# Summing h11 in PSUM: the first product's bank is copied into the second's, and the second product accumulates on the copy

## The chip, the cores and the metric

The kernel runs on one core of one Trainium2 chip. The metric is the device time of one execution in microseconds (us), the median of several runs.

## The reference

Attention over channels is followed by a feed-forward network. For each of 4 batches, q, k and v are 6080 x 256 arrays.

```python
qn = q / (norm(q, axis=1) + 1e-06)          # norm over the 6080 rows
kn = k / (norm(k, axis=1) + 1e-06)
s = kn.transpose(0, 2, 1) @ qn / tau        # 256 x 256 in each batch
a = softmax(s)                              # over the last axis
x = (v @ a).reshape(24320, 256)
h = x @ w_in                                # w_in 256 x 2048
g = maximum(0.01 * h, h)
out = g @ w_out                             # w_out 2048 x 256
```

The result is 24320 x 256. Everything is float32 outside the chip.

## The kernel before, in words

**What is multiplied.** The kernel first works out, for each batch, the product of the attention matrix with w_in (W). Then h comes from v and W with the seven products of Strassen's scheme in Winograd's form, and out comes from g and w_out. Each float32 operand is split into a high and a low half, and each product is three matmuls (`PASSES`): high by high, low by high, high by low. For the first batch the halves are 32 bits wide, later they are float16.

**Tiles and pairs.** The columns of v are worked in 24 tiles (`i`), six in each batch, of 2 x 512 columns and, for the last two of a batch, 2 x 496. In each tile there are eight pairs (`p`). A pair computes four blocks of h, which are named C11, C12, C21 and C22. Tile 0 has an order of its own, tiles 1 to 14 are the conventional tiles of this document, and tiles 15 to 23 (`FAST`) are worked by another function, `fast_slot`.

**One conventional pair.** TensorE does seven block products of three matmuls each (`block_product`, L1193) into two PSUM banks, x and z, of which there is one each:

```python
block_product(i, p, x, A11, "B11", True, False)
h11 = taken(i, x)
block_product(i, p, y, A12, "B21", True, True)
...
add(i, h11, y)
...
block_product(i, p, x, S2, "T2", False, False)
h12 = taken(i, x)
...
block_product(i, p, z, S1, "T1", True, False)
```

In these tiles y is bank z too. The text calls the products by their second operands: B11, B21, T2, T1, T3, T4, B22, in that order. B11, T2, T3 and T4 run into bank x one upon the other; B21 into z; T1 into z from zero; and B22 upon T1. `taken` (ScalarE, L1230) copies bank x into an SBUF tile h. `add` (VectorE, L1224) adds bank z to h. So h11 is the copy of x after B11 plus z after B21; h22 is the copy of x after T3 plus z after T1; h12 is the copy of x after T2 plus z after B22; and C21 is read from x itself after T4. `leaky` (ScalarE L1207 twice, or L1207 and L1213 for C21; VectorE L1217) makes g and its two halves.

**The order of the work.** Each engine's order is written out by hand: `run` and `in_order` keep instructions of one engine in the order of the program. The products of g by w_out of the pair before (`ffn_out`, L1604, 24 matmuls in a pair, six for each of C11, C22, C21 and C12) are put between the block products by `out(n)`, n matmuls at a time: 5, 5, 8 and the remaining 6. Work of other parts of the kernel (scores and norms of later batches, W, splits of v, conversions) waits in lists, and `slot(list, room)` takes entries from the front of a list as long as their written lengths fit in the room. The room that is left over in a slot of ScalarE or VectorE is carried to the next in tiles 6 to 14, up to 0.6. In a conventional pair VectorE has slots of 1.45 (between the h11 addition and C11), 2.2 (between C11 and the h22 addition), 1.45 (between the h22 addition and C22) and 0.8 (at the end).

**fast_slot.** Tiles 15 to 23 copy bank x into bank z after B11 (L1517, ScalarE) and let B21 accumulate on the copy. The matmuls of the pair before that stand between are `out(6)`.

Of the kernel before, what the change touches and what calls it, by code (L numbers as in the profile page):

```python
# [14 lines left out]
AF = mybir.ActivationFunctionType  # L15
# [22 lines left out]
G_SCALE = 2.0**-19  # L38
# [5 lines left out]
def channel_attention_ffn(  # L44
# [17 lines left out]
    nc = tc.nc  # L62
# [10 lines left out]
    widths = [TW] * (N // TILE)  # L73
# [4 lines left out]
    NT = len(widths)  # L78
    NPAIR = NF // 2
    WPB = NT * NPAIR  # L80
    NTILES = B * NT
    T16 = NT
    LEAN = 2
    UNIT = 3
    FAST = range(NTILES - NT - EARLY, NTILES)
# [9 lines left out]
    def bank(tag, bufs=1):  # L95
        return psum.tile([P, TW], F32, name="ps_" + tag, tag=tag, bufs=bufs)
# [37 lines left out]
    issued = {}  # L134

    @contextmanager
    def in_order(*engines):
        with ExitStack() as stack:
            for e in engines:
                if e in issued:  # L140
                    stack.enter_context(tc.issue_after(issued[e].ins))
            yield

    def run(engine, fn, *args):
        with in_order(engine):
            issued[engine] = ins = fn(*args)
        return ins

    def f32(ap):
        return ap if ap.dtype == F16 else ap.bitcast(F32)  # L150

    def pair_type(i):
        return F16 if i >= T16 else F32R
# [105 lines left out]
    class Scores:  # L259
# [95 lines left out]
        def unit(self, j, t):  # L355
            return nc.vector.tensor_tensor(out=t, in0=self.chunk(j), in1=self.rows, op=ALU.mult)
# [447 lines left out]
    S1, S2, S3, S4, A22, A12, A11 = range(NS)  # L804
# [30 lines left out]
    now, w_done, w_stores = [0], {}, []  # L835
# [352 lines left out]
    def block_product(i, p, ps, a, name, first, last):  # L1188
        w, sp = w_split[i, p], v_split[i, name]
        n = widths[i % NT]  # L1190
        with in_order("pe"):
            for k, (x, y) in enumerate(PASSES):
                mm = nc.tensor.matmul(  # L1193
                    out=ps[:, 0:n], lhsT=w[:, x, a, :], rhs=sp[:, y, 0:n],
                    start=first and k == 0, stop=k == 2, skip_group_check=True,
                )
        issued["pe"] = mm

    def leaky(i, p, name, h):

        n = widths[i % NT]
        out = work.tile([P, TW], F32, name="g", bufs=3)
        sp = work.tile([P, 2, TW], pair_type(i), name="g_split", bufs=GBUFS)
        g_split[i, p, name] = sp
        with in_order("act"):
            def unit(to):
                return nc.scalar.activation(  # L1207
                    out=to, in_=h[:, 0:n], func=AF.Prelu, alpha=0.01, scale=G_SCALE if i >= T16 else 1.0
                )

            unit(out[:, 0:n])
            if name == "C21":
                issued["act"] = nc.scalar.copy(out=sp[:, 0, 0:n], in_=out[:, 0:n])  # L1213
            else:
                issued["act"] = unit(sp[:, 0, 0:n])
        with in_order("dve"):
            issued["dve"] = nc.vector.tensor_tensor(  # L1217
                out=sp[:, 1, 0:n], in0=out[:, 0:n], in1=f32(sp[:, 0, 0:n]), op=ALU.subtract
            )

    def add(i, h, ps):
        n = widths[i % NT]
        with in_order("dve"):
            issued["dve"] = nc.vector.tensor_tensor(out=h[:, 0:n], in0=ps[:, 0:n], in1=h[:, 0:n], op=ALU.add)  # L1224

    def taken(i, ps):
        n = widths[i % NT]
        h = temp(name="h")
        with in_order("act"):
            issued["act"] = nc.scalar.copy(out=h[:, 0:n], in_=ps[:, 0:n])  # L1230
        return h
# [357 lines left out]
    def ffn_out(i, p):  # L1589
# [8 lines left out]
        for name, f, j in (("C11", f1, 0), ("C22", f2, 1), ("C21", f2, 0), ("C12", f1, 1)):  # L1598
# [35 lines left out]
    todo = {"act_end": deque(), "dve_add": deque(), "act_first": deque(), "dve_first": deque(), "dve_end": deque(), "dve_idle": deque(), "act": deque(), "dve": deque(), "pe": deque(), "pe_late": deque(), "pe_next": deque(),  # L1634
            "act_next": deque(), "act_late": deque()}
# [8 lines left out]
    def slot(queue, room):  # L1644
        engine = queue.split("_")[0]
        lists = (queue,)
        spots[0] += queue == "pe"
        if queue == "act":
            lists = ("act_first", "act")
        if queue == "dve":  # L1650
            lists = ("dve", "dve_first") if now[0] % NPAIR > 4 else ("dve_first", "dve")
            lists = ("dve_add", *lists) if now[0] // NPAIR in FAST else ("dve_add", *lists, "dve_idle")
        if queue in carried:
            room += carried[queue]
        while True:
            for of in lists:
                if todo[of] and todo[of][0][0] <= room and todo[of][0][1].ready():
                    break
            else:
                if queue in carried and T16 <= now[0] // NPAIR < FAST[0]:  # L1660
                    carried[queue] = min(room, carried["most"])
                return
            length, fn = todo[of].popleft()
            room -= length
            with in_order(engine):
                ins = fn()
            issued[engine] = ins
# [753 lines left out]
    def out(n):  # L2421

        while n and outs:
            if next(outs[0], outs) is outs:
                outs.pop(0)
            else:
                n -= 1

    last = None
    for i in range(NTILES):  # L2430
        for p in range(NPAIR):
            now[0] = i * NPAIR + p
            carried.update(act=0.0, dve=0.0)
            for name in ("pe", "act"):
                todo[name].extend(todo[name + "_next"])
                todo[name + "_next"].clear()
            for fn, args in steps.get(i * NPAIR + p, ()):
                fn(*args)
            if i in FAST:
                assert (i // NT, p) in w_done   # L2440
                fast_slot(i, p)
                continue
            if p:
                w_split.pop((i, p - 1))
            x, y, z = bank("x"), bank("z" if i else "y"), bank("z")
            block_product(i, p, x, A11, "B11", True, False)
            h11 = taken(i, x)
            block_product(i, p, y, A12, "B21", True, True)
            slot("act", 0.65 if i else 0.75 if p else 1.5)
            slot("act_late", 0.65)  # L2450
            add(i, h11, y)
            if last is not None:
                leaky(i, p - 1, "C12", last)
                last = None
            slot("dve", 1.45 if i else 1.3)
            out(5)
            slot("pe", 1 if i and len(todo["pe"]) < 2 else 3)
            if i:
                leaky(i, p, "C11", h11)
            slot("dve", 2.2 if i else 2.6 if p < NPAIR - 1 else 1.5)  # L2460
            slot("act_end", 0.65)
            slot("dve_end", 1.5)
            assert (i // NT, p) in w_done
            block_product(i, p, x, S2, "T2", False, False)
            h12 = taken(i, x)
            if i == 0:
                leaky(i, p, "C11", h11)
                slot("dve", 1.0)
            if i:
                slot("act", 1.8)  # L2470
            block_product(i, p, z, S1, "T1", True, False)
            out(5)
            slot("pe", 1 if i or p else 2)
            block_product(i, p, x, S3, "T3", False, False)
            h22 = taken(i, x)
            add(i, h22, z)
            if i == 0:
                slot("act", 2.2)
            slot("dve", 1.45 if i else 2.8)
            slot("act_end", 0.65)  # L2480
            slot("dve_end", 1.5)
            out(8)
            slot("act_first", 0.65)
            slot("pe", (1 if i >= T16 else 0) if i or p else 2)
            slot("pe_late", 1)
            if i == 0:
                slot("act", 0.6)
            else:
                leaky(i, p, "C22", h22)
            block_product(i, p, x, A22, "T4", False, True)  # L2490
            block_product(i, p, z, S4, "B22", False, True)
            add(i, h12, z)
            leaky(i, p, "C21", x)
            slot("act", 0.65 if i else 0.75)
            slot("act_late", 0.65)
            slot("dve", 0.8)
            if i == 0:
                leaky(i, p, "C22", h22)
                slot("dve", 1.5)
            if i or p == NPAIR - 1:  # L2500
                leaky(i, p, "C12", h12)
            else:
                last = h12
            out(24)
            outs.append(ffn_out(i, p))
    while outs:
# [32 lines left out]
```

## Time and profile before

| | us |
|---|---|
| median of 3 runs (2042.54 to 2043.57) | 2043.02 |
| the profiled execution | 2044.9 |
| its span, first to last instruction | 2043.1 |
| TensorE busy in the span | 2031.6 |
| VectorE busy | 1735.6 |
| ScalarE busy | 1552.8 |

The granted TensorE clock is 1.000 of full speed over the span. A matmul's busy time counts from its start to its modelled end, and matmuls overlap: one of 128x512 lasts 0.38 us in the records while the next starts 0.216 us after it. So an idle time of TensorE is shown only beyond the first 0.16 us of a late start.

### The profile page before, as it was taken

Reading aid. Unit: us, or ns where it says so; the run is one execution under the profiler, and the core shown is the slowest. Engines: PE = TensorE matmul, PEld = TensorE weight load, DVE = VectorE, ACT = ScalarE, POOL = GpSimd, SP = SyncE. Lnnn points to the kernel's source line nnn. Section 1 sums busy time; section 2 is a strip of 40 time slices with the busy share of each in tenths; the row PEclk is TensorE's granted clock in tenths of the full one; section 3 lists DMA queues with packets and bytes.
Section 4 is the critical chain, followed back from the end, with each engine's and each line's share of the span. In section 5 each row is a group of like instructions: output and inputs, shape, how many; then the busy total and the mean of one; then the engine's idle time right before and its main releaser. Section 6 shows DMA issues by size and latency. Waiting matters only on the chain.

```text
span 2043.1 us, 28038 instructions
## 1 busy us (share of the span) xinstructions
PE 2031.6 (99%) x9522; PEld 1183.4 (58%) x9522; DVE 1735.6 (85%) x3187; ACT 1552.8 (76%) x2866; POOL 338.0 (17%) x431
## 2 busy tenths in 40 slices
PE   9999999999999999999999999999999999999999
PEld 8888888888875555544445555444444444444444
DVE  7988888877788887788798888888989988988976
ACT  6567777766668888877766666678988888898886
POOL 0000000000010222210010000013433433333342
PEclk9999999999999999999999999999999999999999
DMA  9946676544764977642333331225778877777774
GB/s 353 406 165 209 203 239 213 195 150 168 233 185 158 276 193 193 165 122 66 109 110 128 110 102 32 69 82 129 150 145 185 173 149 136 155 149 142 139 135 95
DMA packets 146816, 332.89 MB, mean 163 GB/s; under 512 B 16848, under 2 KB 48336, under 8 KB 146672
## 3 DMA queue, kind: packets, MB, share of 16 engines
q1 hardware_dynamic: 92912, 218.61, 31.7%
q0 software_dynamic: 53536, 112.29, 27.4%
q8 instruction: 75, 1.23, 0.2%
q14 instruction: 69, 0.57, 0.1%
q10 hardware_dynamic: 224, 0.20, 0.0%
HBM read 188.74 MB, written 57.42 MB: 120 GB/s over the span
## 4 chain that ended last, share of the span: by engine, by line
PE 94%; DVE 3%; ACT 2%; issue 1%; DMA 0%; ACTq 0%; DVEq 0%
PE ps_o L1604 28%; PE ps_x L1193 23%; PE ps_z L1193 17%; PE ps_o L1330 11%; PE ps_s L404 4%; PE ps_y L1330 2%; PE ps_s L1330 2%; PE ps_o L404 2%; PE ps_s L1956 1%; PE ps_y L404 1%; DVE h L1224 1%; ACT g L1207 1%; ACT g_split L1207 1%; PE ps_y L1956 0%; DVE g_split L1217 0%
## 5 line engine op out<-in xcount | busy, mean ns | idle before, releaser
L1604 PE MATMUL ps_o<-g_split,w_out_split 128*128 128x512 f16 (+3 forms) x2880 | 709.3, 382 | 0.0
L1193 PE MATMUL ps_x<-v_split,w_split 128*128 128x512 f16 (+3 forms) x2280 | 620.1, 381 | 2.5 <-ACT h L1230 2.4
L1193 PEld LDWEIGHTS <-w_split 128*128 128x128 f16 x3024 | 292.5, 98 | 350.0 <-issue 15.6
L1193 PE MATMUL ps_z<-v_split,w_split 128*128 128x512 f16 (+3 forms) x1704 | 461.7, 380 | 2.5 <-DVE h L1224 2.0
L1224 DVE TENSOR_TENSOR h<-ps_z,h 128x512 f32<-128x512 f32 (+1 forms) x497 | 339.6, 683 | 136.4 <-ACT h L1230 118.4
L1230 ACT COPY h<-ps_x 128x512 f32<-128x512 f32 (+1 forms) x505 | 291.1, 576 | 162.6 <-PE ps_x L1193 157.2
L1217 DVE TENSOR_TENSOR g_split<-g,g_split 128x512 f16<-128x512 f32 (+3 forms) x480 | 329.0, 686 | 79.8 <-ACT g_split L1207 74.8
L1207 ACT ACTIVATE g<-h 128x512 f32<-128x512 f32 (+1 forms) x360 | 225.2, 626 | 156.6 <-DVE h L1224 154.0
L1604 PEld LDWEIGHTS <-w_out_split 128*128 128x128 f16 x1728 | 168.8, 98 | 201.9 <-issue 0.5
L1604 PEld LDWEIGHTS ps_o<-g_split,w_out_split 128*128 128x128 f32 x1152 | 216.6, 188 | 43.3
L1207 ACT ACTIVATE g_split<-h 128x512 f16<-128x512 f32 (+3 forms) x360 | 220.2, 612 | 0.0
L1289 DVE TENSOR_TENSOR g_pair<-g_b,g_pair 128x512 f16<-128x512 f32 (+1 forms) x214 | 139.3, 679 | 43.2 <-ACT g_pair L1284 42.8
L1330 PE MATMUL ps_o<-g_pair,w_out_split 128*128 128x512 f16 (+1 forms) x630 | 173.0, 377 | 0.8 <-DVE g_pair L1289 0.4
L1330 PEld LDWEIGHTS <-spare 128*128 128x128 f16 x840 | 82.0, 98 | 97.2 <-issue 0.7
L1284 ACT CAST g_pair<-g_b 128x512 f16<-128x512 f32 (+1 forms) x214 | 123.2, 610 | 0.0
L1193 PEld LDWEIGHTS ps_x<-v_split,w_split 128*128 128x128 f32 x576 | 107.9, 188 | 22.3 <-ACT g L1207 0.4
L1330 PEld LDWEIGHTS <-w_out_split 128*128 128x128 f16 x630 | 61.5, 98 | 73.0 <-issue 0.5
L1289 DVE TENSOR_TENSOR g_pair<-g_a,g_pair 128x512 f16<-128x512 f32 (+1 forms) x144 | 97.4, 677 | 1.5 <-ACT g_pair L1284 0.8
L1139 DVE SCALAR_TENSOR_TENSOR v_split<-v_raw,v_scale,v_split 128x512 f16<-128x512 f32 (+1 forms) x125 | 93.1, 745 | 3.4
L283 POOL MEMSET qk_raw<- 64x512 f32 x5 | 3.0, 591 | 535.5 <-ACT sq L309 267.7
L1284 ACT CAST g_pair<-g_a 128x512 f16<-128x512 f32 (+1 forms) x144 | 88.1, 612 | 2.3
L1296 POOL DMA_DIRECT2D g_a<-g_a x70 | 63.0, 901 | 157.5 <-DVE g_pair L1289 138.0
(278 smaller groups left out, 2712.3 us busy)
## 6 DMA issues: line engine op xcount, KB each, us to landing
w_split<-w_dram SPq DMA_DIRECT2D x40, 896.0 KB, 4.5
qk_raw<-in_q_dram SPq DMA_DIRECT2D x115, 256.0 KB, 4.6
qk_raw<-in_k_dram SPq DMA_DIRECT2D x115, 256.0 KB, 4.3
v_raw<-in_vT_dram SPq DMA_DIRECT2D x32, 512.0 KB, 4.9
out_dram<-o_sb SPq DMA_DIRECT2D x64, 256.0 KB, 3.2
w_split<-w_dram SPq DMA_DIRECT2D x32, 448.0 KB, 4.8
spare<-spare POOLq DMA_DIRECT2D x23, 512.0 KB, 5.2
g_a<-g_a POOLq DMA_DIRECT2D x40, 256.0 KB, 3.3
```

The costliest lines, as they stand in the source:

```text
L404: mm = nc.tensor.matmul(out=out, lhsT=lhsT, rhs=rhs, start=start, stop=stop, skip_group_check=True)
L1139: return nc.vector.scalar_tensor_tensor(out=sp[:, 1, 0:w], in0=src, scalar=up, in1=sp[:, 0, 0:w], op0=ALU.mult, op1=ALU.subtract)
L1193: mm = nc.tensor.matmul(out=ps[:, 0:n], lhsT=w[:, x, a, :], rhs=sp[:, y, 0:n], start=first and k == 0, stop=k == 2, skip_group_check=True,)
L1207: return nc.scalar.activation(out=to, in_=h[:, 0:n], func=AF.Prelu, alpha=0.01, scale=G_SCALE if i >= T16 else 1.0)
L1217: issued["dve"] = nc.vector.tensor_tensor(out=sp[:, 1, 0:n], in0=out[:, 0:n], in1=f32(sp[:, 0, 0:n]), op=ALU.subtract)
L1224: issued["dve"] = nc.vector.tensor_tensor(out=h[:, 0:n], in0=ps[:, 0:n], in1=h[:, 0:n], op=ALU.add)
L1230: issued["act"] = nc.scalar.copy(out=h[:, 0:n], in_=ps[:, 0:n])
L1284: return nc.scalar.copy(out=sp[:, 0, 0:n], in_=g32[i, p, HELD.get(name, name)][:, 0:n])
L1289: return nc.vector.tensor_tensor(out=sp[:, 1, 0:n], in0=g32[i, p, HELD.get(name, name)][:, 0:n], in1=sp[:, 0, 0:n], op=ALU.subtract)
L1296: return nc.gpsimd.dma_start(out=g32[i, p, to][:, 0:n], in_=g32[i, p, of][:, 0:n], accum_op=ALU.add)
L1330: issued["pe"] = nc.tensor.matmul(out=ps[:, 0:n], lhsT=fast_lhsT(i, p, prod, x), rhs=sp[:, y, 0:n], start=p == 0 and k == 0, stop=ends and ...
L1604: issued["pe"] = nc.tensor.matmul(out=o_ps[i][j][h][:, 0:n], lhsT=wo_lhsT(i, x, f, h), rhs=sp[:, y, 0:n], start=p == 0 and early and k == ...
```

## The change

In tiles 1 to 14:

- `seed` puts a ScalarE copy from bank x to bank z in the place of `taken`, and B21 accumulates on it (not from zero). The VectorE addition for h11 goes. Where a tile begins that is wider than the one before it (tiles 6 and 12, first pair), the old way is kept.
- Six matmuls of `ffn_out` and the slots of ScalarE and TensorE come between B11 and B21; T2 follows B21 with nothing between.
- `leaky` of C11 reads bank z; between its two ScalarE instructions stands the copy of h12, and the second is a copy of the first's result.
- `leaky` of C12 is moved from the end of a pair to behind the seed of the next.
- VectorE's slots of 1.45 and 2.2 become 2.1 and 2.2. The matmuls of `ffn_out` go 6, 5, 7 and the remaining 6.
- Slots of lists that only `FAST` tiles fill are dropped.

```diff
-    def leaky(i, p, name, h):
+    def leaky(i, p, name, h, then=None):
...
+        run("act", unit, out[:, 0:n])
+        between = then() if then else None
+        if name == "C21" or then:
+            run("act", lambda: nc.scalar.copy(out=sp[:, 0, 0:n], in_=out[:, 0:n]))
+        else:
+            run("act", unit, sp[:, 0, 0:n])
...
+    def seed(i, p, x, z):
+        n = widths[i % NT]
+        if p == 0 and n > widths[(i - 1) % NT]:
+            return taken(i, x)
+        run("act", lambda: nc.scalar.copy(out=z[:, 0:n], in_=x[:, 0:n]))
...
+            seeded = i > 0
+            x, y, z = bank("x"), bank("z" if i else "y"), None if seeded else bank("z")
             block_product(i, p, x, A11, "B11", True, False)
-            h11 = taken(i, x)
+            h11 = seed(i, p, x, y) if seeded else taken(i, x)
+            if seeded:
+                z = y
+                if last is not None:
+                    leaky(*last)
+                    last = None
+                slot("act", 0.65)
+                slot("act_late", 0.65)
+                out(6)
+                slot("pe", 1 if len(todo["pe"]) < 2 else 3)
+                block_product(i, p, z, A12, "B21", h11 is not None, True)
+                if h11 is not None:
+                    add(i, h11, z)
+                slot("dve", 2.1)
+                block_product(i, p, x, S2, "T2", False, False)
+                h12 = leaky(i, p, "C11", z if h11 is None else h11, lambda: taken(i, x))
+                slot("dve", 2.2)
                 slot("act", 1.8)
+                out(5)
+                block_product(i, p, z, S1, "T1", True, False)
+                slot("pe", 1)
...
             block_product(i, p, x, S3, "T3", False, False)
             h22 = taken(i, x)
             add(i, h22, z)
...
-            out(8)
+            out(7 if seeded else 8)
...
-            if i or p == NPAIR - 1:
+            if i == 0 and p < NPAIR - 1 or seeded and (i, p) != (FAST[0] - 1, NPAIR - 1):
+                last = i, p, "C12", h12
+            else:
                 leaky(i, p, "C12", h12)
```

## Rows read from the trace of the kernel before

**Rows 1.** The page: busy time, share of the span and instructions of each engine.

```profile
PE 2031.6 (99%) x9522; PEld 1183.4 (58%) x9522; DVE 1735.6 (85%) x3187; ACT 1552.8 (76%) x2866; POOL 338.0 (17%) x431
```

**Rows 2.** Busy time in ten stretches: PE, PEld, DVE, ACT, POOL (instructions), clock, DMA.

```profile
0.00:180.60 180.60, 178.93 (x797) 151.30 (x798) 154.69 (x304) 113.36 (x188) 1.75 (x8) 1.00 0.78 288
180.60:597.00 416.40, 416.16 (x1855) 346.42 (x1854) 342.31 (x624) 294.48 (x531) 3.24 (x6) 1.00 0.60 198
...
1029.00:1114.00 85.00, 82.81 (x418) 40.58 (x417) 76.86 (x153) 60.36 (x122) 9.03 (x14) 1.00 0.37 126
...
1386.00:1420.00 34.00, 32.35 (x143) 13.80 (x142) 29.69 (x67) 27.45 (x54) 12.07 (x15) 1.00 0.57 139
1420.00:2020.00 600.00, 599.80 (x2817) 274.89 (x2815) 528.58 (x958) 519.12 (x961) 230.74 (x269) 1.00 0.75 149
```

**Rows 3.** Whom TensorE waited for, 180.6 to 1386 us: total, times, longest.

```profile
PE ps_x L1193 <- ACT h L1230: 2.0, 4, 0.7
PE ps_z L1193 <- DVE h L1224: 1.6, 3, 1.0
```

**Rows 4.** Timeline of TensorE, 955 to 958 us: start, length, instruction, idle before it.

```profile
956.41 0.79 PE L1193 MATMUL ps_x<-v_split,w_split 128*128 128x496 f16 x3 [0.41 <-ACT h L1230]
957.25 0.79 PE L1193 MATMUL ps_z<-v_split,w_split 128*128 128x496 f16 x3
```

**Rows 5.** Timeline, 1028 to 1048 us: B22 waits for the h22 addition.

```profile
1036.88 0.79 PE L1193 MATMUL ps_x<-v_split,w_split 128*128 128x496 f16 x3
...
1038.00 0.67 DVE L1224 TENSOR_TENSOR h<-ps_z,h 128x496 f32<-128x496 f32 x1
...
1038.72 0.79 PE L1193 MATMUL ps_z<-v_split,w_split 128*128 128x496 f16 x3 [1.05 <-DVE h L1224]
```

**Rows 6.** Groups of instructions, 180.6 to 1386 us: busy, mean ns, idle before and releaser.

```profile
L1224 DVE TENSOR_TENSOR h<-ps_z,h 128x512 f32<-128x512 f32 (+1 forms) x336 | 229.6, 683 | 111.7 <-ACT h L1230 100.0 <-PE ps_z L1193 10.1 <-issue 0.2
L1207 ACT ACTIVATE g<-h 128x512 f32<-128x512 f32 (+1 forms) x337 | 210.7, 625 | 155.9 <-DVE h L1224 153.3
L1230 ACT COPY h<-ps_x 128x512 f32<-128x512 f32 (+1 forms) x336 | 193.0, 574 | 138.2 <-PE ps_x L1193 136.9
L1213 ACT CAST g_split<-g 128x512 f16<-128x512 f32 (+3 forms) x112 | 69.0, 616 | 3.6
L1207 ACT ACTIVATE g<-ps_x 128x512 f32<-128x512 f32 (+1 forms) x112 | 66.0, 589 | 9.5 <-PE ps_x L1193 7.4 <-ACT g_split L1207 0.2
```

**Rows 7.** The copy from bank x to bank z in tiles 15 to 23, by its line.

```profile
L1517 ACT COPY ps_z<-ps_x x71: 557/570/581, 1386.1 to 2017.3; 128x512 f32<-128x512 f32 x39, 128x496 f32<-128x496 f32 x32
...
  PE ps_z L1193: 0.2, 1
```

**Rows 8.** Timeline of one pair of tile 2, 283.2 to 294.2 us, all engines.

```profile
283.27 0.84 PE L1193 MATMUL ps_z<-v_split,w_split 128*128 128x512 f32 x3
283.47 0.59 ACT L1230 COPY h<-ps_x 128x512 f32<-128x512 f32 x1 [0.16 <-PE ps_x L1193]
283.96 0.62 ACT L1886 CAST win_t<-win_s 128x512 fp32r<-128x512 f32 x1
...
289.08 0.69 DVE L1224 TENSOR_TENSOR h<-ps_z,h 128x512 f32<-128x512 f32 x1 [0.59 <-ACT h L1230]
289.69 0.68 DVE L1874 TENSOR_TENSOR win_s<-win 128x512 f32<-128x512 f32 x1
289.81 0.63 ACT L1207 ACTIVATE g<-h 128x512 f32<-128x512 f32 x1 [0.76 <-DVE h L1224]
...
290.34 0.62 ACT L1207 ACTIVATE g_split<-h 128x512 fp32r<-128x512 f32 x1
...
290.75 0.84 PE L1193 MATMUL ps_z<-v_split,w_split 128*128 128x512 f32 x3
```

**Rows 9.** Timeline of TensorE, one pair of tile 9 (float16 halves), 914 to 925 us.

```profile
914.79 0.81 PE L1193 MATMUL ps_z<-v_split,w_split 128*128 128x512 f16 x3
...
921.91 0.81 PE L1193 MATMUL ps_z<-v_split,w_split 128*128 128x512 f16 x3
```

More of the change, by code (lines that the diff above doesn't have):

```diff
@@ L1204, in leaky, with unit @@
         g_split[i, p, name] = sp
[L1205 to L1215, printed above, removed]
+        def unit(to):
+            return nc.scalar.activation(
+                out=to, in_=h[:, 0:n], func=AF.Prelu, alpha=0.01, scale=G_SCALE if i >= T16 else 1.0
+            )
+        run("act", unit, out[:, 0:n])
[4 more added lines that the diff above has]
+            run("act", unit, sp[:, 0, 0:n])
         with in_order("dve"):
@@ L1219, in leaky @@
             )
+        return between
+    def seed(i, p, x, z):
[3 more added lines that the diff above has]
+        run("act", lambda: nc.scalar.copy(out=z[:, 0:n], in_=x[:, 0:n]))
     def add(i, h, ps):
@@ L2444, in channel_attention_ffn @@
                 w_split.pop((i, p - 1))
-            x, y, z = bank("x"), bank("z" if i else "y"), bank("z")
+            assert (i // NT, p) in w_done
+            seeded = i > 0
+            x, y, z = bank("x"), bank("z" if i else "y"), None if seeded else bank("z")
             block_product(i, p, x, A11, "B11", True, False)
-            h11 = taken(i, x)
-            block_product(i, p, y, A12, "B21", True, True)
-            slot("act", 0.65 if i else 0.75 if p else 1.5)
-            slot("act_late", 0.65)
@@ L2451, in channel_attention_ffn @@
[L2451 to L2469, printed above, removed]
-                slot("act", 1.8)
-            block_product(i, p, z, S1, "T1", True, False)
-            out(5)
-            slot("pe", 1 if i or p else 2)
+            h11 = seed(i, p, x, y) if seeded else taken(i, x)
[15 more added lines that the diff above has]
+                slot("dve", 2.2)
+                slot("act", 1.8)
+                out(5)
+                block_product(i, p, z, S1, "T1", True, False)
+                slot("pe", 1)
+            else:
+                block_product(i, p, y, A12, "B21", True, True)
+                slot("act", 0.65 if i else 0.75 if p else 1.5)
+                slot("act_late", 0.65)
+                add(i, h11, y)
+                if last is not None:
+                    leaky(*last)
+                    last = None
+                slot("dve", 1.45 if i else 1.3)
+                out(5)
+                slot("pe", 1 if i and len(todo["pe"]) < 2 else 3)
+                if i:
+                    leaky(i, p, "C11", h11)
+                slot("dve", 2.2 if i else 2.6 if p < NPAIR - 1 else 1.5)
+                block_product(i, p, x, S2, "T2", False, False)
+                h12 = taken(i, x)
+                if i == 0:
+                    leaky(i, p, "C11", h11)
+                    slot("dve", 1.0)
+                if i:
+                    slot("act", 1.8)
+                block_product(i, p, z, S1, "T1", True, False)
+                out(5)
+                slot("pe", 1 if i or p else 2)
@@ L2479, in channel_attention_ffn @@
             slot("dve", 1.45 if i else 2.8)
-            slot("act_end", 0.65)
-            slot("dve_end", 1.5)
-            out(8)
+            out(7 if seeded else 8)
             slot("act_first", 0.65)
@@ L2499, in channel_attention_ffn @@
                 slot("dve", 1.5)
-            if i or p == NPAIR - 1:
+            if i == 0 and p < NPAIR - 1 or seeded and (i, p) != (FAST[0] - 1, NPAIR - 1):
+                last = i, p, "C12", h12
+            else:
                 leaky(i, p, "C12", h12)
-            else:
-                last = h12
             out(24)
```

## The prediction

> **What bounds the kernel now.** The page comes first: TensorE is busy for 2031.6 us of a span of 2043.1, VectorE for 85% and ScalarE for 76% [rows 1]. All that any change of order can win is TensorE's idle time, 11.5 us, and what is hidden inside its busy time. The table of stretches says where the idle time lies [rows 2]: 1.7 us in the first stretch, ahead of the change; 0.2 us in 180.6 to 597, where VectorE is busy for 82%; 2.2 us in 1029 to 1114, where it is busy for 90%; 1.65 us where tile 15 begins; and 0.2 us in the 600 us after 1420, which the change does not touch. The waits tell what ended the idle time in tiles 1 to 14 [rows 3]: copies of bank x (2.0 us) and additions of bank z (1.6 us).
>
> That is not the whole loss, since the first 0.16 us of each late start doesn't show as idle. In [rows 4] T2 waits for the copy of h11, 0.41 us shown; three matmuls later T1 starts 0.84 us after T2, where three matmuls of this width take 0.62, so it is 0.2 us late with nothing shown. Counting late starts so, on the timeline from 180.6 to 1386, I find 15 that wait for h11 (T2 for its copy, T1 for its addition, B21 for bank z), 3.4 us in all, the first at 183.57 and the last at 1377.81; and six that wait for h22 (T4 for its copy, B22 for its addition), 3.5 us, of which the one in [rows 5] alone is 1.2. In the first 34 us of tile 15 they come to 3.5 us. So 10.4 us are within reach.
>
> **The change part by part.**
>
> *The h11 addition goes.* There are 112 pairs in tiles 1 to 14, and two keep the old way, so 110 additions of 683 ns [rows 6] go: 75 us of VectorE. VectorE does not set the end, so this is worth what its lateness cost: T1 no longer waits for an addition, and T2 no longer for a copy that stands behind C12 on ScalarE, since C12 now comes after the seed. I take the whole 3.4 us off (bounds 0 and 3.4).
>
> *The copy goes to bank z.* It takes 570 ns in tiles 15 to 23 [rows 7] against 574 ns into SBUF [rows 6]. What is new is that B21 waits for it. Its cover is the six matmuls in front: in the pair of [rows 8], bank x is copied from 283.47, so the seed is done at 284.04, and B21 would start at 283.27 + 6 x 0.227 = 284.63 (33 matmuls lie between 283.27 and 290.75, 0.227 us each). That leaves 0.6 us for ScalarE to be late, and each matmul of the slot now ahead of B21 adds to it. The nearest row is the wait for the copy in tiles 15 to 23, 0.2 us in 71 [rows 7]; for 110 that is 0.3 us, which I take (bounds 0 and 5, a twentieth of a microsecond in each pair).
>
> *C11 on ScalarE.* Its first instruction reads PSUM (589 ns for 625) and its second becomes a copy (616 ns, like L1213) [rows 6]. ScalarE's sum stays as it is, and it now waits for other engines anyway, 153 us for additions [rows 6]. Nothing is taken for this.
>
> *Bank z is read by ScalarE before T1 may begin.* In the pair of [rows 8], reckoned from issue to issue on ScalarE (0.49 after a copy, 0.53 after L1207): seed 283.47, C12 at 283.96 and 284.49, one entry of other work at 285.02, C11's read at 285.55 to 286.14. T1 would come at 284.63 + 11 x 0.227 = 287.12, with a margin of 1.0 us. I take nothing; two further entries ahead of C11 would use the margin up. The Trainium skill (Perfetto Trace Analysis, Matmuls) speaks against this step: independent groups of matmuls should rotate through the PSUM banks, so that the reading of one overlaps the next group. Before, T1 too came into the bank that B21 had used, and waited for VectorE there. By that rule the reading would stand uncovered between B21 and T1; it is the third rival.
>
> *C11 ends later, and with it the VectorE work up to the h22 addition.* This is the cost that I weigh most. In the same pair, with both early slots full: C12 is done on ScalarE at 285.10, its subtraction on VectorE starts at 285.13, and VectorE issues every 0.61 us (289.08 to 289.69 [rows 8]). Three entries in the slot of 2.1 lead to 287.57, C11's subtraction to 288.18, three entries in the slot of 2.2 to 290.01, and the h22 addition ends 0.69 later, at 290.70. B22 is due at 290.75. The margin, now 290.75 - 289.77 = 0.98 us, falls to 0.05: the deferred C12 and the longer slot use up more than the removed addition gave. With float16 halves a pair without other TensorE work has B22 due 7.12 us after the present start of B21 [rows 9], where the reckoning above needs 7.43: 0.31 us late with full slots. On the timeline 37 of the 112 pairs have no more than 7.5 us here, 21 like [rows 8] and 16 like [rows 9]. Bounds: nothing, and 16 x 0.31 + 21 x 0.56 (one entry more than reckoned) = 16.7 us. Full slots are not the rule: from 180.6 to 597 VectorE is busy 8.4 us in a pair of 10.2, and seven instructions of 0.685 are the pair's own, so 3.6 us of other work meet rooms of 6.55. I take one third of the 16: 1.6 us. The six waits for h22 that exist I leave as they are (bounds: all 3.5 go, or they are in the 16.7).
>
> *The entry of tile 15.* VectorE is busy there for 29.7 us of 34 [rows 2], with splits of W left over from tile 14. Rooms that are larger by 0.65 us in each pair take such work earlier. Of the 3.5 us I take a third off, 1.1 (bounds 3.5 off and 2 on, since work that is pulled forward may also meet tile 14 earlier).
>
> Sum: -3.4 + 0.3 + 1.6 - 1.1 = -2.6 us. The profiled execution took 2044.9 us (span 2043.1 and 1.8 around it), so it would take 2042.3; the median of the runs shown is 2043.02, so the forecast is 2040.4. A measurement of this kernel can tell about 0.2%, 4.1 us, from no change, so this counts as no change.
>
> **The rivals.**
>
> *The freed VectorE time spreads.* Besides h11's waits, those of tile 15 go as well, because its leftover work is done by then: -3.4 - 3.5 + 0.3 = -6.6, 2036.4 us; with part of the waits for h22, less. For it speaks that each place with idle time has VectorE at 87 to 90% [rows 2]; against it that work on W and the scores is a chain over three engines, which VectorE's room alone doesn't shorten.
>
> *B22 waits for the h22 addition.* Half of the upper bound, 8.4 us: -3.4 + 0.3 + 8.4 = +5.3, 2048.3 us. It decides for slower from 7.2 us on, that is 0.19 us late in each of the 37 pairs. For it speaks the margin of 0.05 us worked out above; against it the 3.6 us of work for 6.55 us of room.
>
> *T1 waits until ScalarE has read bank z.* If ScalarE runs two entries later than reckoned in a tenth of the pairs, 11 waits of 0.5 us give back what was won: 2043 to 2046 us. Against it stands the margin of 1.0 us.
>
> *The change doesn't do what it says.* The old way remains in two pairs of 112, so this is not counted.
>
> **How the numbers follow.** The forecast has 0.50, with a range of its own from 2039 to 2044; the first rival 0.30, the second 0.15, the third 0.05. Faster by over 0.2% (under 2038.9) is the first rival and the edge of the forecast, 0.33; slower (over 2047.1) is the second and a little of the third, 0.16; the rest, 0.51, is no change that can be told. The range from 2036 to 2047.5 leaves out the far ends of the first two rivals, some 0.2.
>
> **What would show it.** TensorE's instructions and busy time per matmul stay as they are. The additions at L1224 number 110 fewer, ScalarE's waits for them fall from 153 us, and the waits of T2 and T1 in 944 to 1114 and around 1299 and 1377 are gone. VectorE's additions for h22 end close ahead of B22 in pairs like [rows 8]. If I am wrong, it shows as new idle time of TensorE at bank z: behind a VectorE addition (second rival), behind a ScalarE read of z (third) or behind the seed.

## The result, and the profile after

The changed kernel took 2067.22 us (median of 4 runs, 2066.54 to 2069.81) against 2043.01 in the same session: ratio 1.0121, 95% interval 1.0103 to 1.0138. It is 24.2 us slower. The forecast was 2040.4, the range 2036 to 2047.5.

The page comes first, with the engines' busy time in its order of [rows 1].

```profile
PE 2037.5 (99%) x9522; PEld 1180.9 (57%) x9522; DVE 1658.5 (80%) x3077; ACT 1547.5 (75%) x2866; POOL 338.2 (16%) x431
```

VectorE has 110 instructions fewer and is busy for 77 us less than in [rows 1], which is what the change takes away. The span nevertheless grew from 2043.1 to 2065.2. So the loss lies in order and waits, and the stretches say where. They are those of [rows 2], the last two moved by the 21 us that tile 15 now begins later.

```profile
0.00:180.60 180.60, 178.83 (x804) 151.25 (x805) 156.63 (x307) 115.53 (x191) 1.75 (x8) 1.00 0.78 292
180.60:597.00 416.40, 413.57 (x1826) 339.47 (x1826) 311.46 (x590) 284.37 (x523) 3.56 (x5) 1.00 0.60 199
1029.00:1114.00 85.00, 81.83 (x430) 41.91 (x429) 69.77 (x133) 58.24 (x117) 5.52 (x8) 1.00 0.30 102
1407.00:1441.00 34.00, 32.94 (x147) 14.04 (x146) 27.02 (x58) 25.88 (x48) 8.53 (x10) 1.00 0.47 101
1441.00:2041.00 600.00, 598.99 (x2812) 274.90 (x2811) 528.58 (x958) 518.24 (x960) 230.87 (x269) 1.00 0.75 149
```

Ahead of the change nothing moved, and behind it TensorE is idle for 1.0 us where it was 0.2. In the second stretch TensorE is idle for 2.8 us where it was 0.2, although VectorE there is busy for 75% instead of 82%. The entry of tile 15 improved, from 1.65 us idle to 1.06. The rest is in tiles 1 to 14. TensorE's waits there (180 to 1405 us; total, times, longest) answer to [rows 3].

```profile
PE ps_z L1193 <- DVE h L1233: 8.8, 20, 1.1
PE ps_x L1193 <- ACT h L1239: 7.4, 8, 1.6
PE ps_z L1193 <- ACT ps_z L1228: 2.4, 1, 2.4
```

Every wait of T2 and T1 for h11 is gone. In their place B22 waits in bank z for the h22 addition (L1233), T4 in bank x for h22's copy (L1239), and B21 once for the seed (L1228). Counted as late starts of the products of h, as the prediction counts (distance from start to start over the usual one, from 60 ns up), B22 is late 38 times, 14.6 us in all, and T4 ten times, 9.1 us; before the change B22 was late four times, 1.9 us, and T4 twice, 1.6 us. All such late starts of tiles 1 to 14 come to 29 us, against 7 before. These 22 us are the loss.

Why does an engine with 77 us less work finish later? Its waits ahead of the subtraction that makes a half low (L1218; the group, then who ended the idle time: us, times).

```profile
L1218 DVE TENSOR_TENSOR g_split<-g,g_split x480: 634/684/694, 91.9 to 1407.4; 128x512 f16<-128x512 f32 x75, 128x512 fp32r<-128x512 f32 x43, 128x496 fp32r<-128x496 f32 x21, 128x496 f16<-128x496 f32 x21
...
  ACT g_split L1207: 171.6, 149
  ACT g_split L1214: 65.7, 73
```

The same line before the change (L1217 there):

```profile
  ACT g_split L1207: 74.8, 147
```

VectorE stands for 237 us at these subtractions until ScalarE has written the high half, where it stood for 75. Not all of this is new idle time: at the additions it stood for 111.7 us before [rows 6] and now for 48.3 (180 to 1405 us).

```profile
L1233 DVE TENSOR_TENSOR h<-ps_z,h 128x512 f32<-128x512 f32 (+1 forms) x225 | 153.2, 681 | 48.3 <-ACT h L1239 44.1 <-PE ps_z L1193 3.8
```

What counts is where it stands. C12's subtraction now comes first in the pair, and C11's behind h12's copy. Behind a waiting instruction nothing else of VectorE runs. The Trainium skill (PSUM — Partial Sum Buffer, Engine vs sequencer instructions) calls the queues of ScalarE and VectorE strictly first in, first out; the trace agrees: in the pair shown next VectorE runs nothing in its waits of 1.35 and 0.89 us.

One pair with float16 halves shows both waits and what they push back (timeline, all engines).

```profile
659.80 0.58 ACT L1228 COPY ps_z<-ps_x 128x512 f32<-128x512 f32 x1
...
661.49 0.69 DVE L1218 TENSOR_TENSOR g_split<-g,g_split 128x512 f16<-128x512 f32 x1 [1.35 <-ACT g_split L1207]
...
661.76 0.82 PE L1193 MATMUL ps_z<-v_split,w_split 128*128 128x512 f16 x3
...
662.10 1.41 DVE L1160 TENSOR_TENSOR v_raw<-v_raw 128x512 f32<-128x512 f32 x2
...
663.27 0.58 ACT L1239 COPY h<-ps_x 128x512 f32<-128x512 f32 x1
663.75 0.62 ACT L1214 CAST g_split<-g 128x512 f16<-128x512 f32 x1
...
664.40 0.69 DVE L1218 TENSOR_TENSOR g_split<-g,g_split 128x512 f16<-128x512 f32 x1 [0.89 <-ACT g_split L1214]
...
665.84 0.57 ACT L1239 COPY h<-ps_x 128x512 f32<-128x512 f32 x1
...
666.96 0.81 PE L1193 MATMUL ps_x<-v_last,w_split 128*128 128x512 f16 x3
...
667.46 0.68 DVE L1233 TENSOR_TENSOR h<-ps_z,h 128x512 f32<-128x512 f32 x1
...
668.20 0.38 PE L1193 MATMUL ps_z<-v_split,w_split 128*128 128x512 f16 x1 [0.44 <-DVE h L1233]
```

Read from the top: VectorE waits 1.35 us for C12's second write, does two entries, waits 0.89 us for C11's cast, and then has four entries (665.01 to 667.46) ahead of the h22 addition. T4 starts at 666.96, so B22 was due 0.64 later, at 667.60; the addition ends at 668.14. The copy of h22 (665.84) had long been there: only VectorE's order made B22 late.

T4's waits come from ScalarE. Another pair, same view.

```profile
1108.45 0.61 ACT L1214 CAST g_split<-g 128x496 f16<-128x496 f32 x1
...
1110.87 0.68 DVE L356 TENSOR_TENSOR unit<-qk_raw,spare 128x512 f32<-128x512 f32 x1
...
1111.59 0.62 ACT L362 CAST qk_split<-unit 128x512 f16<-128x512 f32 x1 [2.53 <-DVE unit L356]
1112.11 0.56 ACT L1239 COPY h<-ps_x 128x496 f32<-128x496 f32 x1
...
1112.73 0.79 PE L1193 MATMUL ps_x<-v_split,w_split 128*128 128x496 f16 x3 [1.01 <-ACT h L1239]
```

An entry of ScalarE's slot (the cast L362) needs what an entry of VectorE's slot makes (L356), and that one stands behind C11's late subtraction. ScalarE idles 2.53 us, with h22's copy behind the cast; T4 waits for that copy. Such waits of L362 come to 15.0 us in nine places, against 6.7 in seven before.

### The profile page after: what moved, and what is told of

It reads as the page before. It is cut to its first block, busy times and chain, and to the rows that moved or that the text cites. A ratio compares the mean times of both kernels' runs of the same rounds, so it can differ in the third digit from the quotient of the medians.

```text
span 2065.2 us, 27833 instructions
## 1 busy us (share of the span) xinstructions
PE 2037.5 (99%) x9522; PEld 1180.9 (57%) x9522; DVE 1658.5 (80%) x3077; ACT 1547.5 (75%) x2866; POOL 338.2 (16%) x431
## 4 chain that ended last, share of the span: by engine, by line
PE 87%; DVE 6%; ACT 4%; issue 2%; DMA 1%; POOL 0%; SPq 0%; ACTq 0%; POOLq 0%
PE ps_o L1613 25%; PE ps_x L1193 21%; PE ps_z L1193 16%; PE ps_o L1339 10%; PE ps_s L404 4%; PE ps_s L1339 2%; PE ps_y L1339 2%; PE ps_o L404 2%; DVE g_split L1218 1%; DVE h L1233 1%; PE ps_s L1965 1%; ACT g_split L1214 1%; PE ps_y L404 1%; ACT h L1239 1%; DVE v_split L1139 1%
## 5 line engine op out<-in xcount | busy, mean ns | idle before, releaser
L1218 DVE TENSOR_TENSOR g_split<-g,g_split 128x512 f16<-128x512 f32 (+3 forms) x480 | 328.2, 684 | 239.4 <-ACT g_split L1207 171.6
L1233 DVE TENSOR_TENSOR h<-ps_z,h 128x512 f32<-128x512 f32 (+1 forms) x387 | 263.8, 682 | 73.6 <-ACT h L1239 62.6
L1239 ACT COPY h<-ps_x 128x512 f32<-128x512 f32 (+1 forms) x395 | 229.0, 580 | 102.5 <-PE ps_x L1193 92.2
L1207 ACT ACTIVATE g<-h 128x512 f32<-128x512 f32 (+1 forms) x250 | 156.9, 627 | 119.9 <-DVE h L1233 119.8
L1207 ACT ACTIVATE g_split<-h 128x512 f16<-128x512 f32 (+3 forms) x248 | 152.2, 614 | 0.0
L1214 ACT CAST g_split<-g 128x512 f16<-128x512 f32 (+3 forms) x232 | 143.1, 617 | 3.7
L1207 ACT ACTIVATE g<-ps_z 128x512 f32<-128x512 f32 (+1 forms) x110 | 65.0, 591 | 64.8 <-PE ps_z L1193 64.3
L1228 ACT COPY ps_z<-ps_x 128x512 f32<-128x512 f32 (+1 forms) x110 | 62.5, 569 | 55.4 <-PE ps_x L1193 45.7
```

Of the source, the lines that this page charges most:

```text
L1207: return nc.scalar.activation(out=to, in_=h[:, 0:n], func=AF.Prelu, alpha=0.01, scale=G_SCALE if i >= T16 else 1.0)
L1214: run("act", lambda: nc.scalar.copy(out=sp[:, 0, 0:n], in_=out[:, 0:n]))
L1218: issued["dve"] = nc.vector.tensor_tensor(out=sp[:, 1, 0:n], in0=out[:, 0:n], in1=f32(sp[:, 0, 0:n]), op=ALU.subtract)
```

## The experiments

Theory A: it is the order. What stands ahead of h22's copy and of its addition, waits and entries, makes T4 and B22 late. Theory B: the sum in PSUM itself, the seed or the occupied bank z, costs the time. All were timed against the kernel before; ratios are to it. The late starts are counted as above, in tiles 1 to 14; those behind a matmul of the scores (L404) are left out. In the column of bank x, T4 itself is 1.4 to 1.9 us in e5, e6, e7, e9 and e10, and most of the rest is B11.

| kernel | median us | ratio, 95% interval | B22 late, us | bank x behind other work (T4), us | bank z behind other work (B21, T1), us |
|---|---|---|---|---|---|
| changed | 2067.2 | 1.0121, 1.0103 to 1.0138 | 14.6 | 9.1 | 2.7 |
| e1_room_later | 2057.1 | 1.0071, 1.0056 to 1.0086 | 1.9 | 10.1 | 2.3 |
| e2_c12_at_end | 2075.1 | 1.0158, 1.0141 to 1.0175 | 10.1 | 8.5 | 11.5 |
| e3_h11_in_sbuf | 2116.4 | 1.0359, 1.0344 to 1.0375 | 42.9 | 21.0 | 0.7 |
| e4_c12_low_later | 2062.0 | 1.0092, 1.0077 to 1.0107 | 11.5 | 9.1 | 2.0 |
| e5_h22_copy_first | 2061.6 | 1.0090, 1.0075 to 1.0105 | 16.2 | 3.8 | 0.8 |
| e6_both_rooms | 2051.1 | 1.0040, 1.0026 to 1.0054 | 0.9 | 3.2 | 6.6 |
| e7_three | 2049.6 | 1.0028, 1.0016 to 1.0040 | 0.3 | 2.3 | 5.4 |
| e8_seed_old_order | 2127.8 | 1.0414, 1.0399 to 1.0430 | (T1) 74.6 | 0.2 | 7.7 |
| e9_dve_room_late_tiles | 2043.7 | 1.0001, 0.9992 to 1.0011 | 0.3 | 2.8 | 1.3 |
| e10_seed_first_late_tiles | 2046.9 | 1.0018, 1.0008 to 1.0027 | 0.6 | 3.0 | 2.6 |
| e11_before_rooms | 2059.1 | 1.0074, 1.0059 to 1.0089 | (B21, T1, B22) 10.0 | (T2, T4) 9.2 | 0.5 |
| e12_sbuf_three | 2086.2 | 1.0209, 1.0193 to 1.0224 | 32.1 | 2.9 | 0.6 |

**e1_room_later.** VectorE's room is moved from ahead of the h22 addition to behind it.

```diff
-                slot("dve", 2.2)
+                slot("dve", 1.5)
...
-            slot("dve", 1.45 if i else 2.8)
+            slot("dve", 2.25 if i else 2.8)
```

> The changed kernel with 0.7 us of VectorE's room moved from ahead of the h22 addition to behind it (slots 2.1, 1.5 and 2.25 for 2.1, 2.2 and 1.45). Theory A: the loss comes from the h22 addition, which stands on VectorE behind C12's and C11's subtractions and 4.3 us of slots, so that B22 and T4 wait; then most of the 24 us go, some 2045 to 2053 us. Theory B: the loss comes from the sum in PSUM itself (B21 waits for the copy, bank z is held until ScalarE has read it); then nothing changes, 2065 to 2069 us.

B22's late starts nearly vanish and 10.2 us come back; 2057.1 lies between the two expectations. The rooms ahead of the h22 addition are now 3.6 in all; the kernel before had 3.65, the changed one 4.3. T4's late starts stay: a move on VectorE alone doesn't empty ScalarE's queue ahead of h22's copy. One of them, 3.6 us at 1038.5, stands behind a cast (L362) that waited 4.4 us for a store.

**e2_c12_at_end.** C12 goes back to the end of its own pair.

```diff
-            if i == 0 and p < NPAIR - 1 or seeded and (i, p) != (FAST[0] - 1, NPAIR - 1):
+            if i == 0 and p < NPAIR - 1:
```

> The changed kernel with C12 back at the end of its pair, as before the change (its ScalarE and VectorE work stands ahead of the next seed). Theory A, in the form that VectorE's idle time ahead of the deferred C12 subtraction is what makes the h22 addition late: 2045 to 2055 us, and the seed, now behind C12 on ScalarE, makes B21 wait in some pairs. Theory B: slower than the change, 2067 to 2080 us, since the seed comes later.

Slower by 7.8 us than the change; theory A in this form had 2045 to 2055. B22 gains 4.5 us, but the seed now stands behind C12's two writes: in bank z 11.5 us of late starts instead of 2.7. (In each of the two sums one start, 3.6 and 2.5 us, stands behind a cast L862 that waits for a store.) VectorE's idle time ahead of the subtractions stays at 230 us; it only waits for C11 (157 us) instead of C12. The deferral is a help.

**e3_h11_in_sbuf.** The new order without the sum in PSUM: h11 copied to SBUF and added in every pair.

```diff
-        if p == 0 and n > widths[(i - 1) % NT]:
-            return taken(i, x)
-        run("act", lambda: nc.scalar.copy(out=z[:, 0:n], in_=x[:, 0:n]))
+        return taken(i, x)
```

> The changed kernel's order of work, but h11 is summed the old way in all pairs: copied to SBUF, B21 from zero, VectorE addition. Theory A: the order is what costs, and VectorE has 110 additions more ahead of the h22 addition, so as slow as the change or slower, 2066 to 2085 us. Theory B: the sum in PSUM is what costs, so near the kernel before, 2040 to 2048 us.

2116.4, 49 us above the changed kernel and beyond the 2066 to 2085 of theory A. In this order the sum in PSUM saves 49 us, and the order with its larger rooms, without the sum, costs 73. Theory B falls in its plain form.

**e4_c12_low_later.** C12's subtraction stands behind VectorE's first slot, so that entries run while ScalarE still writes.

```diff
+                    low12 = leaky(*last, later=True)
...
                 slot("dve", 2.1)
+                if low12 is not None:
+                    low12()
```

> The changed kernel with VectorE's subtraction for the deferred C12 moved behind the slot of 2.1, so that VectorE takes other work while ScalarE makes C12. Theory A: the idle time ahead of that subtraction (some 1 us in a pair) is filled, the h22 addition ends earlier by up to as much, 2045 to 2056 us. Theory B: no change, 2065 to 2069 us.

5.3 us come back, 3.1 of them at B22; 2062.0 lies between the two expectations. The idle time at the subtractions falls only from 237 to 200 us.

**e5_h22_copy_first.** ScalarE's room is moved behind h22's copy, from tile 5 on.

```diff
-                slot("act", 1.8)
+                if i < 5:
+                    slot("act", 1.8)
...
             add(i, h22, z)
+            if i > 4:
+                slot("act", 1.8)
```

> Only ScalarE's room of 1.8 is moved: from ahead of h22's copy to behind it, from tile 5 on. If ScalarE's list entries ahead of h22's copy are what T4 waits for (9 late starts in bank x, some 9 us, in the changed kernel), these waits fall below 3 us and the time to about 2060; the waits of B22 for the h22 addition (14.6 us) stay or shrink little, because the addition is VectorE's. If T4 waits because T3 itself, or the copy of h12, comes late, the waits stay and the time stays at 2067.

The late starts in bank x fall from 9.1 to 3.8 us, T4's own to 1.9 (the rest is B11's); B22's don't fall. 5.6 us come back. T4's waits were ScalarE's entries.

**e6_both_rooms.** e1 and e5 together.

> VectorE's room (as in the first experiment) and ScalarE's room both moved behind h22. If order is the whole loss, the two gains add: 2057 minus some 7, about 2050, with less than 5 us of late starts in T4 and B22 together. If entries pushed behind h22 come back as waits of the next pair's seed and of B21, the time stays at 2055 or more and late starts appear ahead of B21.

16.1 us come back, where the two alone gave 10.2 and 5.6: they add. What is left in bank z (6.6 us) is mostly one wait of 4.5 us, early in tile 14.

**e7_three.** e1, e4 and e5 together.

> Both rooms behind h22 and the delayed subtraction of C12 behind VectorE's first room, so that VectorE has other work while ScalarE writes C12's high half. If VectorE's idle time ahead of C12's and C11's subtractions is what makes the h22 addition late, this is the fastest of all: 2043 to 2048. If the three only move the same wait around, it is no faster than the second experiment of this set.

The median is 2049.6, 1.5 better than e6 and just above the 2043 to 2048 expected. T4 and B22 are late by 1.7 us in all. The one wait of B21 remained: ScalarE's cast L862 waits 4.9 us for a store of an earlier part of the weights, with the seed behind it. It costs more than its length (stretches of TensorE alone: busy, clock, DMA).

```profile
1298.00:1301.90 3.90, 0.00 (x1) 0.97 0.69 271
1301.90:1304.90 3.00, 2.98 (x8) 0.50 0.00 0
1306.00:1308.00 2.00, 2.00 (x11) 1.00 0.00 0
```

After 3.9 us without a matmul the granted clock is at 0.50, the lower level of 1.2 GHz, for the next 3 us, which loses another 1.5.

**e8_seed_old_order.** The sum in PSUM alone, in the order of the kernel before: C12 at the end of its pair, both writes of C11 read from bank z ahead of h12's copy. Against the kernel before, only outputs and TensorE's slot move ahead of B21, and VectorE's early room is 2.1. The edit is shown against the changed kernel.

```diff
-                if last is not None:
-                    leaky(*last)
-                    last = None
                 slot("act", 0.65)
                 slot("act_late", 0.65)
-                out(6)
+                out(5)
...
+                if last is not None:
+                    leaky(*last)
+                    last = None
                 slot("dve", 2.1)
+                leaky(i, p, "C11", z if h11 is None else h11)
+                slot("dve", 2.2)
                 block_product(i, p, x, S2, "T2", False, False)
-                h12 = leaky(i, p, "C11", z if h11 is None else h11, lambda: taken(i, x))
-                slot("dve", 2.2)
+                h12 = taken(i, x)
                 slot("act", 1.8)
+                block_product(i, p, z, S1, "T1", True, False)
                 out(5)
-                block_product(i, p, z, S1, "T1", True, False)
...
-            out(7 if seeded else 8)
+            out(8)
...
-            if i == 0 and p < NPAIR - 1 or seeded and (i, p) != (FAST[0] - 1, NPAIR - 1):
+            if i == 0 and p < NPAIR - 1:
```

> The sum in PSUM alone, in the order of the kernel before: C12 at the end of its pair, both writes of C11 ahead of h12's copy, VectorE's rooms where they were; only the list entries of TensorE and the outputs move ahead of B21, which gives the seed its time. If the new order and not the sum in PSUM costs the time, this stays within 10 us of the kernel before (2033 to 2053). If the sum in PSUM costs by itself (B21 behind the seed, C11 behind B21, T1 behind both reads of bank z), it is 2060 or more, with late starts at B21 and T1.

2127.8, outside what theory A allowed. TensorE's waits (180 to 1450 us) name the place.

```profile
PE ps_z L1193 <- ACT g_split L1207: 55.2, 108, 0.6
PE ps_z L1193 <- ACT ps_z L1228: 6.5, 9, 3.5
```

And one of them on TensorE's timeline: B21, T2, then T1.

```profile
653.91 0.82 PE L1193 MATMUL ps_z<-v_split,w_split 128*128 128x512 f16 x3
654.57 0.81 PE L1193 MATMUL ps_x<-v_split,w_split 128*128 128x512 f16 x3
655.91 0.81 PE L1193 MATMUL ps_z<-v_split,w_split 128*128 128x512 f16 x3 [0.53 <-ACT g_split L1207]
```

T1 starts a new sum in bank z, where ScalarE still reads C11, twice, and only T2 lies between. This is the third rival, at full size, in an order that doesn't cover it. It is the rule of the Trainium skill (Perfetto Trace Analysis, Matmuls) that groups should rotate through the banks; the trace agrees here with 55.2 us of waits. The changed kernel pays next to nothing for it (T1 is late once, 0.1 us): there C11's second write reads `g` in SBUF, and five outputs stand between T2 and T1. So the sum does have a price, and the new order is what avoids it.

**e9_dve_room_late_tiles.** e7, with VectorE's late room back at 1.6 from tile 13 on.

```diff
-            slot("dve", 2.25 if i else 2.8)
+            slot("dve", (2.25 if i < 13 else 1.6) if i else 2.8)
```

> The three edits, with VectorE's room behind the h22 addition back at 1.6 instead of 2.25 from tile 13 on, where the weights' halves ran ahead of their stores: there a weight cast of ScalarE (L862) waited 4.9 us for a store, and the seed behind it kept B21 waiting 3.9 us. If it is the list work drawn forward that runs into its own stores, that wait shrinks and the time falls from 2047 to 2050 to some 2042 to 2045. If the wait has another cause, it stays.

2043.7, no difference from before that can be measured. The wait for the store is gone; the longest waits of TensorE in tiles 1 to 14, and VectorE's at the subtractions, are these.

```profile
PE ps_x L1193 <- DVE v_split L1144: 1.1, 1, 1.1
PE ps_z L1193 <- ACT ps_z L1232: 1.1, 1, 1.1
...
  ACT g_split L1214: 130.6, 94
  ACT g_split L1207: 46.5, 53
```

VectorE still stands for 177 us at ScalarE's halves. With the rooms in their place that costs TensorE hardly anything.

**e10_seed_first_late_tiles.** e7, with ScalarE's last slots of a pair moved behind the next pair's seed from tile 13 on.

```diff
-                slot("act", 0.65)
+                slot("act", 0.65 if i < 13 else 1.3)
...
-            slot("act", 0.65 if i else 0.75)
-            slot("act_late", 0.65)
+            if i < 13:
+                slot("act", 0.65 if i else 0.75)
+                slot("act_late", 0.65)
```

> The three edits, and from tile 13 on ScalarE's last list entries of a pair moved behind the next pair's seed, so that an entry that waits for a store doesn't stand ahead of a seed. If the seed's place in ScalarE's queue is what costs, B21's wait of 3.9 us goes and the time is 2042 to 2045. If the waiting entry only stops the next thing behind it (C12's writes, h12's copy), the same 4 us appear at T1 or T3 and the time stays at 2047 to 2050.

2046.9, between the two expectations: B21's 3.9 us are gone, but L862 still waits for stores, 2.5 us in two places, and TensorE waits 1.0 us for C11's read ahead of T1, 0.9 for a copy of a weights' product, 0.6 elsewhere. The wait was partly moved on.

**e11_before_rooms.** The kernel before, with e1's and e5's moves.

```diff
-            slot("dve", 2.2 if i else 2.6 if p < NPAIR - 1 else 1.5)
+            slot("dve", 1.5 if i else 2.6 if p < NPAIR - 1 else 1.5)
...
-            if i:
+            if 0 < i < 5:
                 slot("act", 1.8)
...
+            if i > 4:
+                slot("act", 1.8)
-            slot("dve", 1.45 if i else 2.8)
+            slot("dve", 2.25 if i else 2.8)
```

> The kernel before, without the sum in PSUM, with both rooms moved behind h22 as in the sixth experiment. If the rooms behind h22 are a gain for any order, its six late B22 and the T4 waits (3.5 and 2.8 us) go and it is faster than before, 2036 to 2041. If they only repair what the new order does to VectorE and ScalarE, it is no faster: 2042 to 2050.

2059.1: slower, not faster, beyond both expectations. B22 and T4 do gain: they are late by 1.3 us, where the kernel before has 3.5 (four times B22, twice T4). But what stands behind h22 now stands ahead of the next pair's start and of h11: T2, which needs the copy of h11, T1, which needs the addition, and B21 are late by 17.3 us instead of 3.4. The largest of these starts is T2's, 3.6 us.

```profile
1039.12 0.61 ACT L862 ACTIVATE w_first<-w_a 128x128 f16<-128x128 f32 x2 [3.93 <-DMA w_dram<-w_first]
...
1040.65 0.55 ACT L1230 COPY h<-ps_x 128x496 f32<-128x496 f32 x1
...
1041.25 0.79 PE L1193 MATMUL ps_x<-v_split,w_split 128*128 128x496 f16 x3 [3.48 <-ACT h L1230]
```

The copy of h11 stands behind C12's two writes and a cast L862 that waited 3.9 us for a store; from 1042.2 to 1045.2 the granted clock is 0.57. The moves repair the new order, where h11 needs no addition and the seed has six matmuls in front; they are no gain by themselves.

**e12_sbuf_three.** e7's three edits, with h11 in SBUF as in e3.

> The three edits with h11 summed in SBUF: ScalarE's copy to SBUF and VectorE's addition of some 0.68 us in each pair, in the new order. It weighs the sum in PSUM once the order gives h22 its place. If the removed addition is worth something only while VectorE's queue ahead of h22 is full, it is close to the three edits with the seed: 2047 to 2060. If the addition counts wherever it stands in the new order (it cost 49 us with the rooms as the change has them), it is 2085 or more, with late starts at B22.

2086.2, the second expectation: 36.6 above e7, and B22 is late by 32 us. With the order repaired the sum in PSUM still saves 37 us against the addition in the same order.

## Why the prediction was wrong, point by point

The second rival, which had 0.15, happened, beyond the half of its bound at which it was priced and in other pairs than it was argued from, and a part on ScalarE joined it.

*The h11 waits went.* Right: none is left, and the 110 additions are gone.

*The copy to bank z.* 0.3 us was taken; 2.7 us of late starts in bank z were measured, 2.5 of them one place, where a store held up ScalarE. Inside the bounds of 0 and 5.

*T1 and the reads of bank z.* Right for this order at nothing; e8 shows the price where the cover is gone.

*C11 ends later.* This is the step that failed: "I take one third of the 16: 1.6 us", that is, a third of the 16 short pairs like [rows 9] at 0.31 us, and nothing for the 21 like [rows 8]. Measured: B22 is late 38 times, 14.6 us, where it was late four times, 1.9 us. That 14.6 is close to the upper bound of 16.7, and 38 to the 37 pairs that were counted as short, is chance. Some 36 pairs have no more than 7.55 us from B21 to B22 on the trace before; nine of them are late after the change, by 2.1 us. The 21 like [rows 8], 11.8 us of the bound, come to 0.3. And 31 of the 38 late pairs lie in tiles 6 to 14, with 12.9 us. So the choice inside the bound failed, and so did the choice of the pairs that it was made from.

What the reckoning left out there is the room that is carried in tiles 6 to 14. The four entries behind C11's subtraction in the pair shown have written lengths of 0.5, 0.75, 0.75 and 0.75, together 2.75: with up to 0.6 carried the slot of 2.2 takes them, where three were reckoned. "Full slots are not the rule" rested on an average: 3.6 us of VectorE's other work in a pair against 6.55 us of room. On the changed kernel's timeline the pairs where B22 starts over 0.70 us after T4 have 4.2 instructions of other work between C11's subtraction and the h22 addition, 2.0 us, the others 2.1, 1.1 us. The room ahead of h22 is filled first, not evenly. In how many of the 31 pairs the carried room decides, no run tested.

The reckoning within a pair missed another thing. From the seed to the end of the h22 addition it gives 7.23 us (283.47 to 290.70); the pair shown took 8.34 (659.80 to 668.14). About 0.5 of the difference is C11's subtraction, which waits for a cast that now stands behind h12's copy, 4.60 us after the seed where 4.10 was reckoned; the other 0.6 is a fourth entry. VectorE was treated as running through; it stood 237 us at ScalarE's halves.

*The waits for h22 left as they are.* Also wrong: T4's late starts, 1.6 us before, became 9.1. No step of the prediction followed ScalarE's slot ahead of h22's copy, whose entries wait for VectorE's entries; e5 shows this term by itself, 5.6 us.

*The entry of tile 15.* 1.1 us off was taken; its late starts fell from 3.5 to 2.8 us. They did not go, as the first rival had it.

The sum redone in late starts of tiles 1 to 14, before to after: T2, T1 and B21 for h11 3.4 to none, bank z behind other work (B21 for the seed, T1) none to 2.7, B22 1.9 to 14.6, T4 1.6 to 9.1, T3 none to 0.65, within blocks 0.5 to 2.1. That is 21.8 of the 22.1 us by which the span grew.

Where did the 77 us of VectorE go? Off the critical path. In e9, with nearly every wait for h22 gone, the kernel with the sum in PSUM equals the old one: TensorE is busy for 99% in both, and late starts of some 7 us in tiles 1 to 14, with 3.5 at the entry of tile 15, were all that there was to win. What was not settled: whether a further placing of the slots would bring a measurable gain over the kernel before; e9 is the best that was found. And not every microsecond of e10's loss was followed to an instruction.

## What to carry to other kernels

An operation that is removed from an engine that doesn't set the end is worth its lateness, and the reordering that makes room for it can cost more than that: price the queue of every engine between the moved instructions and the next due date, waits included, and take room as full, with what can be carried into it, where the work ahead of a due date is drawn from a list. A slot of list work belongs behind the instruction that TensorE waits for, not ahead of it, as long as the next due date has cover (e11 shows the price where it has none), and an entry that waits for another engine's entry is dangerous there. When a bound is worked out pair by pair, choose inside it pair by pair too, not by an average over the stretch; and when the measured sum comes near the bound, see whether it comes from the pairs that the bound was made of.

## What was not expected of the hardware

A stall of TensorE of 3.9 us (e7) left the granted clock at 0.50 for the 3 us that followed; in the changed kernel a stall of 2.3 us (1335.8 to 1338.1) left it at 1.00. So in e7 the wait cost more than its own length, and the shorter one did not. ScalarE's copy of 128x512 from bank to bank took 573 ns on average (78 in tiles 1 to 14), its copy to SBUF 583 ns (162): the place of the seed changes its own duration hardly at all.
